# Output products by a seven-product scheme, with its sums on VectorE and a new order of the work

## The chip, the cores and the metric

The kernel runs on one core of one Trainium2 chip. The metric is the time of one execution in device microseconds. Engines are named as in the profile: PE (TensorE matmuls), PEld (its weight loads), DVE (VectorE), ACT (ScalarE), POOL (GpSimd), SP (SyncE, which here only issues DMAs).

## What is computed

Four items (batch entries), eight heads, 768 tokens of 64 values per head, eight blocks of 96 tokens. The reference, cut to what matters:

```python
P = sort_net                                   # 8x8 per head
for _ in range(5):                             # softmax over rows, then columns normalised
    P = exp(P - max(P)); P = P / sum(P, -1); P = P / sum(P, -2)
k_sorted, v_sorted = P @ blocks of k, P @ blocks of v
attn = softmax(q_block @ k_sorted_block.T / 8) # inside each block of 96
x    = attn @ v_sorted_block                   # 3072 tokens x 512
g    = maximum(x @ w1, x @ w2)                 # 3072 x 1024
out  = g @ w_out                               # 3072 x 512, float32
```

## The kernel before, in words

**The maxout is folded into the weights.** `w1_sb` is overwritten with w1 - w2, so that g = relu(x(w1 - w2)) + x w2, and out = relu(x(w1 - w2)) w_out + x (w2 w_out). `w_product` (L654) makes `wc` = w2 w_out once (512x512). Each 128 tokens of output are then twelve matmuls with 128 rows of contraction each: eight with `g` and `wo_sb`, four with `xT` and `wc`, all 512 columns wide (`out_products`, L700).

**Stages of an item b.** `load_k`, `load_q`, `load_v` (L132 to L172) are DMAs issued by POOL, in order, from float32 in memory to bf16 in SBUF. `sort_k` (L449, three calls) multiplies k by a block-diagonal matrix and evacuates to `kT`. `turn_v` (L242) copies v to another layout in `v_dc`, in four pieces of 24 columns. `sort_v_pair` (L516, eight calls, for items 1 and 2 together) and `sort_v_halved` (L493, four calls, for item 3) do for v what `sort_k` does for k. `pair_q` (L403, two DVE copies) and `q_transposes` (L413) make `qT`; for items 2 and 3 the transposes are DMAs on SP's queue. `scores` (L539, eight units u) does eight small matmuls and an exponential on ACT (L556). `values` (L567, eight units) does eight small matmuls and, on DVE, a reciprocal (L586) and a multiplication (L592). `x_transposes` (L600) makes `xT`; for items 1 to 3 these are DMAs on SP. `moe_h` (L685, two halves of 384 tokens, four pairs of 128 rows of g) does eight matmuls with 384 columns and a relu evacuation on ACT or DVE. `moe_out` (L714) does the twelve matmuls of a 128-token tile in two parts of six, evacuates two tiles together, and SP stores them (512 KB). `moe_out_last` (L729) does the last two tiles of the last item, the very last in pieces of 384 and 128 columns.

**PSUM.** One pool of four buffers (L62), each 128x1024 float32, that is two halves of 512 columns. Everything that PE writes takes one of the four, and gives it back when its evacuation has read it.

**The order of the work** is the order in which the program records instructions: each engine runs its own in that order and waits by semaphore. The front (L777 to L844), until item 0's g is there, is a list written out by hand. After it the loop at L915 runs, for each item, its eight `moe_h` units (item 0: none, but four `w_product`), then twelve half tiles of output, and after unit n the steps that `first_tail`, `second_tail`, `third_tail` (L859 to L914) give for n: the next item's attention. Which of ACT and DVE evacuates is chosen by `pick` (L96) from a running account of both, unless the step names one.

Of the kernel before, what the change touches and what calls it, by code (L numbers as in the profile page):

```python
# [10 lines left out]
FP32 = mybir.dt.float32  # L11
# [5 lines left out]
def kernel(  # L17
# [34 lines left out]
    NFB = DFF // 128  # L52
    NE = 8

# [77 lines left out]
    def load_q(b, by_pair=False):  # L132
        if b == 2:
            t = w2_sb.rearrange("p t f -> p (t f)")[:, 0 : H * R * D].rearrange(
                "p (h x) -> p h x", h=H
            )
        elif b == 3:
            t = v_raw[:, HB * D :].rearrange("p (h x) -> p h x", h=H)
        else:
            t = qpool.tile([128, H, R * D], BF16, tag="q_raw", name="q_raw", bufs=1)  # L140
        src = q[b].rearrange("h (p r) d -> p h (r d)", r=R)
        for hs in [slice(hp, H, HP) for hp in range(HP)] if by_pair else [slice(0, H)]:
            nc.gpsimd.dma_start(out=t[:, hs], in_=src[:, hs])
        q_raw[b] = t
# [7 lines left out]
    def load_k(b):  # L152
        k_raw[b] = (
            kpool.tile([128, HB * D], BF16, tag="k_raw", name="k_raw")
            if b < 3
            else v_raw[:, 0 : HB * D]
        )
        n = HB * D // NCH
        for ci in range(NCH):
            nc.gpsimd.dma_start(  # L160
                out=k_raw[b][:, ci * n : (ci + 1) * n],
                in_=k_src[b, :, ci * n : (ci + 1) * n],
            )
# [78 lines left out]
    def turn_v(rows, eng, c0, c1):  # L242
# [6 lines left out]
        else:  # L249
            nc.vector.tensor_copy(  # L250
                out=dst.bitcast(U32).rearrange("p (d c) -> p d c", c=BLK)[:, :, c0:c1],
# [150 lines left out]

    def pair_q(b, two):  # L403

        if two == 0:
            q_pair[b] = qpool.tile([128, HP, R, 2 * D], BF16, tag="q_pair", name="q_pair", bufs=1)
        nc.vector.tensor_copy(
            out=q_pair[b][:, :, :, two * D : (two + 1) * D],
            in_=q_raw[b][:, two * HP : (two + 1) * HP].rearrange("p h (r d) -> p h r d", r=R),
        )  # L410
        load["D"] += 900

# [123 lines left out]

    e_tiles, x_tiles = {}, {}

    def scores(b, u, n=0):  # L539
# [3 lines left out]
        for ii in range(4):  # L543
            i = ih * 4 + ii
            for h2 in range(2):
# [8 lines left out]
                )  # L554
        e = e_bufs[(b * 8 + u) % NE]
        nc.scalar.activation(  # L556
# [96 lines left out]

    def w_product(dmt):  # L654
        ps = ps_f32("wc_ps")
        for fb in range(NFB):
# [6 lines left out]
            )  # L663
        evac(wc[:, dmt, :], ps[:, 0:512], 512)

# [31 lines left out]

    out_ps = {}

    def out_products(dst, b, ti, n0=0, n1=512, part=None):  # L700
        ch, off = divmod(ti * 128, TCH)
        for m in range(NFB + HP) if part is None else range(part * 6, part * 6 + 6):
            hp = m - NFB
            nc.tensor.matmul(  # L704
                dst,
                g_tiles[b, ch, m // 2][:, m % 2, off : off + 128]
                if m < NFB
                else xT[:, b % 2, ch, hp % 2, hp // 2, off : off + 128],
                wo_sb[:, m, n0:n1] if m < NFB else wc[:, hp, n0:n1],
                start=(m == 0),  # L710
                stop=(m == NFB + HP - 1),
            )

    def moe_out(b, ti, part):  # L714
        slot = ti % 2
        if slot == 0 and part == 0:
            out_ps[0] = ps_f32("out_ps")
        ps = out_ps[0]
        out_products(ps[:, slot * 512 : (slot + 1) * 512], b, ti, part=part)
        if slot == 1 and part == 1:  # L720
            tok0 = b * S + ti * 128
            o = opool.tile([128, 2, 512], FP32, tag="o", name="o")
            evac(o.rearrange("p t n -> p (t n)"), ps, 1024)
            nc.sync.dma_start(
                out=out[tok0 - 128 : tok0 + 128, :].rearrange("(t p) n -> p t n", p=128),
                in_=o,
            )

    def moe_out_last(ti, pieces):  # L729

        tok0 = (B - 1) * S + ti * 128
        for n0, n1, eng in pieces:
            ps = ps_f32("out_ps")
            out_products(ps[:, 0 : n1 - n0], B - 1, ti, n0, n1)
            o = opool.tile([128, n1 - n0], FP32, tag=f"o{ti}{n0}", name="o", bufs=1)
            if eng == "A":
                nc.scalar.copy(out=o, in_=ps[:, 0 : n1 - n0])
            else:
                nc.vector.tensor_copy(out=o, in_=ps[:, 0 : n1 - n0])  # L739
            (nc.scalar if eng == "A" else nc.sync).dma_start(  # L740
                out=out[tok0 : tok0 + 128, n0:n1], in_=o
            )


    def att(b):

        SC = [lambda u=u: scores(b, u) for u in range(8)]
        VA = [lambda u=u: values(b, u) for u in range(8)]
        TR = [lambda t=t: x_transposes(b, t) for t in range(4)]
        return SC, VA, TR  # L750

# [94 lines left out]

    def turn(rows, c0):
        turn_v(rows, "D", c0, c0 + 24)
        load["D"] += 850

    def sorts_and_scores(b):
        SC, VA, TR = att(b)
        return SC, VA, TR, [lambda t=t: sort_k(b, t) for t in range(3)]

    SC, VA, TR, KS = sorts_and_scores(1)
    VS = [lambda t=t: sort_v_pair(2, t) for t in range(8)]
    TQ = [lambda half=half: q_transposes(1, half) for half in range(2)]
    TURN = [lambda c=c: turn(both, c) for c in (0, 24, 48, 72)]
    first_tail = {  # L859
        7: KS,  # L860
        9: [TQ[0], TURN[0]],
        10: [SC[0], TQ[1], TURN[1]],
        11: SC[1:4] + TURN[2:4] + [lambda half=half: load_v(3, half=half) for half in range(2)],
        12: VS[0:3],
        13: VS[3:6],
        14: VS[6:8] + [SC[4]],
        15: [VA[0], lambda: pair_q(2, 0)],
        16: [VA[1], lambda: pair_q(2, 1)],
        17: SC[5:8] + [TR[0]],
        18: [VA[2]],  # L870
        19: [VA[3], TR[1]],
        20: [VA[4]],
        21: [VA[5], TR[2]],
        22: [VA[6], VA[7], TR[3]],
    }
    SC, VA, TR, KS = sorts_and_scores(2)
    VS = [lambda t=t: sort_v_halved(3, t) for t in range(4)]
    TURN = [lambda c=c: turn(both, c) for c in (0, 24, 48, 72)]
    second_tail = {
        0: [lambda: q_transposes(2, 0), lambda: q_transposes(2, 1)],  # L880
        2: KS,
        4: SC[0:2],
        5: [VA[0]],
        6: SC[2:4] + [TURN[0]],
        7: [VA[1], TR[0]],
        8: [VA[2], TURN[1]],
        9: [VA[3], TR[1], TURN[2]],
        10: SC[4:7],
        11: [VA[4], TURN[3]],
        12: [VA[5], TR[2], lambda: load_k(3), lambda: load_q(3)],  # L890
        13: [VA[6]],
        14: SC[7:8] + VS[0:2],
        15: [VA[7], TR[3]],
        16: VS[2:4],
        17: [lambda: pair_q(3, 0)],
        18: [lambda: pair_q(3, 1)],
    }
    SC, VA, TR, KS = sorts_and_scores(3)
    third_tail = {
        0: [lambda: q_transposes(3, 0), lambda: q_transposes(3, 1)],  # L900
        2: KS,
        5: SC[0:2],
        6: [VA[0]],
        7: [VA[1], TR[0]],
        8: SC[2:5],
        9: [VA[2]],
        10: [VA[3], TR[1]],
        11: [VA[4]],
        12: SC[5:8],
        13: [VA[5], TR[2]],  # L910
        14: [VA[6]],
        16: [VA[7], TR[3]],
    }
    tails = [first_tail, second_tail, third_tail, {}]  # L914
    for b in range(B):  # L915
        units = [lambda ch=ch, t=t: moe_h(b, ch, t) for ch in range(2) for t in range(4)]
        cost = [13] * 8
        if b == 0:
            units, cost = [lambda: None] * 8, [0] * 8
        if b == 0:  # L920
            units += [lambda dmt=dmt: w_product(dmt) for dmt in range(4)]
            cost += [17] * 4
        units += [
            lambda ti=ti, part=part: moe_out(b, ti, part)
            for ti in range(6 if b < B - 1 else 4)
            for part in range(2)
        ]
        cost += [13] * 12
        if b == B - 1:
            units += [  # L930
                lambda: moe_out_last(4, [(0, 512, "D")]),
                lambda: moe_out_last(5, [(0, 384, "D"), (384, 512, "A")]),
            ]
        for n, unit in enumerate(units):
            elapse(100 * cost[n] if n < len(cost) else 0)
            unit()
            for step in tails[b].get(n, []):
                elapse(250)
                step()
# [28 lines left out]
```

## Time and profile before

| | |
|---|---|
| median of 3 runs | 166.83 us (166.24 to 167.07) |
| span of the profiled execution | 165.0 us |
| PE busy in it | 157.0 us (95%) |
| DVE, ACT, POOL busy | 77.5, 82.3, 33.9 us |
| mean granted TensorE clock | 0.999 |
| `out_ps` matmuls (L704) in the chain that ended last | 37% of the span |

The profiled execution's own time outside its span isn't recorded; the median of the runs is 1.83 us above the span. Busy times of PE are modelled and overlap, so the prediction goes by distances between starts. "a <-b" behind an idle time names what the engine waited for.

### The profile page before, as it was taken

What the parts mean: (1) busy time and instruction counts of PE and PEld (TensorE: products, weight loads), DVE (VectorE), ACT (ScalarE), POOL (GpSimd) and SP (SyncE); (2) the same over time, 40 slices, a digit from 0 to 9 for tenths busy, and PEclk for the clock granted to TensorE, in tenths of its full rate; (3) what the DMA queues carried; (4) which work ended last, traced back from release to release, by engine and by line L of the source; (5) the groups of instructions that cost most, each with busy time, mean ns of one, the idle gap of its engine ahead of it and who ended that gap; (6) DMA issues with size and microseconds to landing.
All of it is one profiled execution on the core that took longest, in us unless ns stands there. A gap on an engine that the chain in (4) does not pass through costs nothing.

```text
span 165.0 us, 4561 instructions
## 1 busy us (share of the span) xinstructions
PE 157.0 (95%) x2007; PEld 95.4 (58%) x2025; DVE 77.5 (47%) x170; ACT 82.3 (50%) x101; POOL 33.9 (21%) x61
## 2 busy tenths in 40 slices
PE   7889999999999999999999999999999999999992
PEld 7839776756554555557655554575655546654451
DVE  4878995684366564525277763250642420000011
ACT  3489776617239846055652353457447206642020
POOL 7949997131206000000014010000000000000000
PEclk9999999999999999999999999999999999999999
DMA  3999999999999999689515999995025294000333
GB/s 41 204 204 194 164 196 207 209 205 220 210 203 204 220 224 167 175 84 228 111 19 104 126 212 157 200 309 29 0 52 175 50 164 142 0 0 0 127 131 127
DMA packets 30404, 23.90 MB, mean 145 GB/s; under 512 B 16752, under 2 KB 25200, under 8 KB 30384
## 3 DMA queue, kind: packets, MB, share of 16 engines
q0 software_dynamic: 11040, 13.37, 50.0%
q1 hardware_dynamic: 19200, 10.17, 28.9%
q8 instruction: 16, 0.26, 0.7%
q10 hardware_dynamic: 144, 0.07, 0.1%
q14 instruction: 4, 0.03, 0.1%
HBM read 26.75 MB, written 6.29 MB: 200 GB/s over the span
## 4 chain that ended last, share of the span: by engine, by line
PE 81%; DMA 6%; DVE 5%; ACT 3%; POOL 2%; issue 2%
PE out_ps L704 37%; PE h_ps L677 25%; DMA w_sb<-in_moe_w_dram 5%; PE wc_ps L657 4%; PE o_ps L575 4%; PE k_ps L458 3%; PE s_ps L548 3%; ACT e L556 1%; POOL w_sb L189 1%; PE v_ps L523 1%; DMA p_sb<-in_sort_net_dram 1%; PE tq_ps L433 1%; DVE colsum L276 1%; DVE p_sb L273 1%; PE tw_ps L638 1%
## 5 line engine op out<-in xcount | busy, mean ns | idle before, releaser
L704 PE MATMUL out_ps<-wo_sb,g 128*128 128x512 bf16 (+2 forms) x187 | 46.0, 370 | 1.4 <-issue 1.0
L677 PE MATMUL h_ps<-xT,w_sb 128*128 128x384 bf16 x256 | 44.5, 326 | 0.0
L677 PEld LDWEIGHTS <-w_sb 128*128 128x128 bf16 x256 | 24.0, 98 | 15.5
L556 ACT ACTIVATE e<-s_ps 96x768 bf16<-96x768 f32 x32 | 24.0, 805 | 14.8 <-PE s_ps L548 14.8
L691 ACT ACTIVATE g<-h_ps 128x768 bf16<-128x768 f32 x27 | 21.7, 811 | 17.4 <-PE h_ps L677 17.3
L704 PEld LDWEIGHTS <-g 128*128 128x128 bf16 x200 | 17.1, 97 | 15.8
L704 PE MATMUL out_ps<-wc,xT 128*128 128x512 bf16 (+2 forms) x98 | 24.7, 370 | 0.1
L108 ACT COPY o<-out_ps 128x1024 f32<-128x1024 f32 x10 | 10.1, 1012 | 28.0 <-PE out_ps L704 25.2
L592 DVE TENSOR_TENSOR x<-o_ps,rs 96x512 bf16<-96x512 f32 x32 | 22.0, 687 | 1.1
L704 PEld LDWEIGHTS <-xT 128*128 128x128 bf16 x100 | 9.6, 97 | 11.2
L575 PEld LDWEIGHTS <-e 96*128 96x128 bf16 x256 | 11.7, 97 | 5.7 <-DVE v_sb L110 0.2
L586 DVE RECIPROCAL rs<-o_ps 96x8 f32<-96x8 f32 x32 | 6.4, 201 | 17.2 <-PE o_ps L575 17.1
L739 DVE COPY o<-out_ps 128x512 f32<-128x512 f32 (+1 forms) x2 | 1.2, 625 | 27.6 <-PE out_ps L704 27.6
L575 PE MATMUL o_ps<-v_sb,e 96*128 96x65 bf16 x256 | 12.7, 193 | 0.0
L110 DVE CAST kT<-k_ps 128x1024 bf16<-128x1024 f32 x6 | 7.2, 1222 | 8.4 <-PE k_ps L458 8.4
L110 DVE CAST v_sb<-v_ps 96x1024 bf16<-96x1024 f32 x7 | 8.5, 1219 | 4.9 <-PE v_ps L523 2.2
L160 POOL DMA_DIRECT2D v_raw<-in_k_dram x3 | 2.5, 838 | 35.1 <-DVE v_dc L250 31.4
L108 ACT CAST v_sb<-v_ps 96x1024 bf16<-96x1024 f32 x9 | 8.8, 1015 | 1.6 <-PE v_ps L500 0.8
L169 POOL DMA_DIRECT2D v_raw<-in_v_dram x11 | 6.5, 593 | 12.7 <-DVE v_dc L250 6.4
L693 DVE TENSOR_SCALAR g<-h_ps 128x768 bf16<-128x768 f32 x5 | 4.8, 957 | 8.9 <-PE h_ps L677 8.8
L548 PEld LDWEIGHTS <-kT 64*128 64x128 bf16 x256 | 6.1, 94 | 4.8 <-issue 2.6
L548 PE MATMUL s_ps<-qT,kT 64*128 64x96 bf16 x256 | 8.5, 204 | 0.3 <-DVE qT L110 0.2
(97 smaller groups left out, 144.4 us busy)
## 6 DMA issues: line engine op xcount, KB each, us to landing
out_dram<-o SPq DMA_DIRECT2D x11, 512.0 KB, 3.4
v_raw<-in_v_dram POOLq DMA_DIRECT2D x8, 384.0 KB, 13.5
k_raw<-in_k_dram POOLq DMA_DIRECT2D x9, 256.0 KB, 11.0
w_sb<-in_moe_w_dram POOLq DMA_DIRECT2D x4, 256.0 KB, 6.0
w_sb<-in_moe_w_dram POOLq DMA_DIRECT2D x2, 512.0 KB, 9.6
wo_sb<-in_moe_w_out_dram POOLq DMA_DIRECT2D x2, 512.0 KB, 13.7
v_raw<-in_v_dram POOLq DMA_DIRECT2D x3, 256.0 KB, 5.0
q_raw<-in_q_dram POOLq DMA_DIRECT2D x4, 192.0 KB, 9.1
```

Of the source, the lines that this page charges most:

```text
L108: nc.scalar.copy(out=out_ap, in_=in_ap)
L110: nc.vector.tensor_copy(out=out_ap, in_=in_ap)
L169: nc.gpsimd.dma_start(out=v_raw[r0 : r0 + 64, m * n : (m + 1) * n], in_=v_src[b, :, m * n : (m + 1) * n],)
L548: nc.tensor.matmul(ps[:, h2 * 512 + ii * 128 : h2 * 512 + ii * 128 + BLK], kT[b][rows, (hp * 8 + i) * BLK : (hp * 8 + i) * BLK + 128], rhs ...
L556: nc.scalar.activation(out=e[:, 0 : 8 * BLK].rearrange("p (t c r) -> p t c r", t=8, r=R), in_=ps[0:BLK] .rearrange("p (t f) -> p t f", t=8 ...
L575: nc.tensor.matmul(ps[:, h2 * 512 + ii * 65 : h2 * 512 + (ii + 1) * 65], e[:, (h2 * 4 + ii) * BLK : (h2 * 4 + ii) * BLK + 128], v_sb[:, m0 ...
L586: nc.vector.reciprocal(out=rs, in_=ov[:, :, :, 64])
L592: nc.vector.tensor_tensor(out=x, in0=ov[:, :, :, 0:D], in1=rs.to_broadcast([BLK, 2, 4, D]), op=ALU.mult,)
L657: nc.tensor.matmul(ps[:, 0:512], w2T[:, fb, dmt * 128 : (dmt + 1) * 128], wo_sb[:, fb, :], start=(fb == 0), stop=(fb == NFB - 1),)
L677: nc.tensor.matmul(h_ps[ch, t][:, m * 512 : m * 512 + TCH], w1_sb[:, hp, fb * 128 : (fb + 1) * 128], xT[:, b % 2, ch, hp % 2, hp // 2, :], ...
L691: nc.scalar.activation(out=g, in_=src, func=AF.Relu)
L704: nc.tensor.matmul(dst, g_tiles[b, ch, m // 2][:, m % 2, off : off + 128] if m < NFB else xT[:, b % 2, ch, hp % 2, hp // 2, off : off + 12 ...
```

## The change

The output rows of an item are split in halves `ch` (tokens 0 to 383, 384 to 767), the contraction of 1536 in halves (`g` pairs 0, 1 and half of `xT`; `g` pairs 2, 3 and the other half), and the 512 output columns in halves of 256 (`NW`). The four quarter products of each are replaced by seven products of sums (Strassen's algorithm, in Winograd's form). With A the left blocks, B the right ones, the sums are

S1 = A21 + A22, S2 = S1 - A11, S3 = A11 - A21, S4 = A12 - S2; T1 = B12 - B11, T2 = B22 - T1, T3 = B22 - B12, T4 = B21 - T2.

T is made once, from `wo_sb` (token `w0.n`, 128x1024 bf16) and `wc` (`w1.n`, 128x512); S for every item, from `xT` (`Xb.n`, 128x768) and from `g` (`Gb.t.n`, t = 0, 1, 128x768). All are tensor_tensor instructions on DVE. A group (class `Group`) has seven steps: `Pb.n` for tiles 0 and 1 of both halves, `Ub.n` for tile 2. It holds one PSUM buffer for all its steps and takes the two halves of it (`bank`) in turn; each step is six matmuls of 256 columns for each tile, and then a copy or an addition of PSUM and SBUF in float32. Stores of a group come after steps 5 and 6.

Other edits: `k_raw` of item 3 is now a buffer of the k pool, `q_raw` of item 3 lies in `v_dc`, and `q_pair` shares the storage of `q_raw`; so loads `lk3` and `lq3` are issued earlier and `lv0`, `lv1` (v of item 3) later, behind `y1`, a POOL copy of a few elements of item 1's `xT`, which waits for all four transposing DMAs of item 1. The exponentials rotate over six buffers and not eight. The order after the front is now one list of tokens: k, q, s, v, x, t, b, p, c, h are `sort_k`, `q_transposes`, `scores`, `values`, `x_transposes`, `turn_v`, sorts of v, `pair_q`, `w_product`, `moe_h` (numbers: item, then unit); a last letter A, D or P names ACT, DVE or POOL. The front is the same.

```diff
-    NE = 8
+    NE = 6
+    NW = DMODEL // 2
...
-            t = v_raw[:, HB * D :].rearrange("p (h x) -> p h x", h=H)
+            t = v_dc[:, 0 : H * R * D].rearrange("p (h x) -> p h x", h=H)
...
+        k_raw[b] = kpool.tile([128, HB * D], BF16, tag="k_raw", name="k_raw")
...
+            q_pair[b] = qpool.tile([128, HP, R, 2 * D], BF16, tag="q_raw", name="q_pair", bufs=1)
...
+    def product(self, bank, lw, rw, new):
+        n = 0
+        last = len(self.ks) * len(self.tiles) - 1
+        for k in self.ks:
+            for p, ti in enumerate(self.tiles):
+                ins = nc.tensor.matmul(
+                    self.ps[:, bank * 512 + p * NW : bank * 512 + (p + 1) * NW],
+                    left(self.b, lw, k, ti * 128), right(rw, k),
+                    start=new and n == 0, stop=n == last, ...)
+                self.apart(ins, bank)
+                n += 1
...
+    def step(self, at, eng):
+        if at == 0:
+            self.ps = ps_f32("out_ps")
...
+            self.product(0, "a11", "b11", True)
+            self.first = self.copy(self.by_tile(self.a), 0, eng)
+        elif at == 1:
+            self.product(1, 2, 2, True)
+            self.second = self.add(1, 0, 1, a, [self.first], eng)
+        elif at == 2:
+            self.product(0, "a12", "b21", False)
+            self.copy(self.part(0, 0), 0, eng)
+        elif at == 3:
+            self.product(1, 1, 1, False)
+            self.third = self.add(0, 1, 1, a, [self.first], eng)
+        elif at == 4:
+            self.product(0, 3, 3, True)
+            self.fourth = self.add(1, 1, 0, self.part(0, 1), [self.third], eng)
+        elif at == 5:
+            self.product(1, 4, "b22", False)
+            self.fifth = self.add(0, 1, 1, a, [self.first, self.fourth], eng)
+            self.store(0)
+        else:
+            self.product(0, "a22", 4, False)
+            self.add(1, 0, 0, self.part(1, 0), [self.first, self.second, self.fifth], eng, True)
+            self.store(1)
...
-    tails = [first_tail, second_tail, third_tail, {}]
-    for b in range(B):
...
+    plan = [
+        """
+        w0.1D k1.0A X0.1D G0.0.1D k1.1A X0.3D G0.1.1D c2D k1.2A lk3 X0.2D G0.0.2D w0.3D q1.0A
+        q1.1D c0D G0.1.3D G0.0.4D s1.0 s1.2 G0.1.2D G0.0.3D t1.0D t1.1D c3A t1.3D s1.4 s1.5
+        t1.2D c1A s1.6 s1.3 P0.0A b2.0A w0.2D w1.1D w1.2D b2.2A b2.7D P0.1D b2.4A b2.3A b2.1D
+        P0.2D b2.6A b2.5D k2.0A k2.1A k2.2A X0.4D w1.3D p2.0A G0.1.4D v1.0 p2.1D P0.3D v1.4 lq3
+        s1.7 q2.0 v1.2 P0.4D s1.1 U0.0A v1.7 U0.1D v1.5 U0.2A v1.6 U0.3D q2.1 v1.3 w0.4D x1.3
+        x1.2 w1.4D U0.4D v1.1 x1.0 x1.1 P0.5D k3.1A y1 P0.6D s2.5 s2.4 U0.5D U0.6D s2.6 s2.7
+        X1.1D lv1 k3.2A k3.0D lv0 h1.1.2D h1.1.1A X1.2D s2.2 s2.0 h1.1.3A p3.0D X1.3D h1.0.2A
+        v2.0 v2.4 h1.0.0A p3.1A G1.1.1D v2.5 h1.0.1A X1.4D x2.2 h1.1.0D G1.1.2D s2.1 s2.3
+        G1.0.1D h1.0.3A v2.1 G1.0.2D v2.7 P1.0A v2.6 U1.0D G1.1.3D G1.0.3D t3.1D P1.1D q3.0 v2.3
+        v2.2 x2.0 U1.1D t3.2D U1.2A q3.1 G1.1.4D P1.2A G1.0.4D P1.3D s3.4 s3.5 P1.4D x2.1 U1.3D
+        s3.7 t3.3D x2.3 s3.2 t3.0D P1.5D P1.6D U1.4D b3.3D s3.1 b3.1A U1.5D U1.6D b3.0D s3.6
+        b3.2D h2.0.2A h2.0.0A v3.5 v3.2 X2.1D h2.1.2A h2.1.3A X2.2D h2.1.0A v3.4 h2.0.1D G2.0.1D
+        h2.1.1A s3.0 G2.0.2D G2.0.4D G2.1.1D G2.1.2D s3.3 P2.0A U2.0A v3.6 v3.3 X2.4D P2.1D
+        h2.0.3A X2.3D U2.1D v3.7 x3.2 P2.2D U2.2A G2.1.3D G2.0.3D v3.1 v3.0 x3.1 x3.3 x3.0
+        G2.1.4D P2.3D P2.4D U2.3D U2.4D P2.5D U2.5D U2.6D P2.6D h3.1.0D h3.0.0A h3.1.2A G3.0.1D
+        h3.1.3A h3.0.1D G3.0.2D h3.1.1A X3.1D G3.0.3D G3.1.1D G3.1.2D h3.0.3A G3.1.3D U3.0D
+        h3.0.2A X3.2D P3.0A P3.1D G3.1.4D U3.1D U3.2D G3.0.4D P3.2A X3.4D X3.3D P3.3D P3.4D
+        U3.3D U3.4D P3.5D P3.6D U3.5D U3.6D
+        """,
+    ]
```

In `Group.add(ch, half, n, other, ...)` the output quarter (ch, half) is set to PSUM half n plus `other`; `apart` removes the ordering between PE's writes into one half of the buffer and reads of the other half.

## The prediction

> **What bounds the kernel now.** First the table by stage: the front ends at 38.4 us, and then come the tails of items 0, 1, 2 and 3 and the end. Columns: the stretch, its length, busy time and count of PE, PEld, DVE, ACT, POOL, then granted clock, DMA share and GB/s.
>
> ```profile
> 38.40:71.10 32.70, 31.88 (x498) 18.16 (x506) 18.34 (x29) 17.07 (x22) 3.55 (x5) 1.00 1.03 202
> 71.10:104.30 33.20, 32.58 (x422) 18.84 (x424) 17.74 (x28) 15.61 (x19) 3.40 (x4) 1.00 0.88 133
> 104.30:135.95 31.65, 31.43 (x359) 17.94 (x361) 11.30 (x21) 15.53 (x19) 0.00 (x0) 1.00 0.61 118
> 135.95:161.95 26.00, 25.86 (x146) 13.87 (x146) 1.25 (x2) 9.52 (x11) 0.00 (x0) 1.00 0.20 74
> 161.95:165.00 3.05, 0.00 (x0) 0.00 (x0) 0.00 (x0) 0.27 (x1) 0.00 (x0) 0.95 0.25 86
> ```
>
> PE is full in all four tails, at full clock; DVE and ACT are half idle. So PE work removed there is time, while DVE has 14 to 25 us per stage to give. Next, the chain of waits, in order of time:
>
> ```profile
> PE 81%; DMA 6%; DVE 5%; ACT 3%; POOL 2%; issue 2%
> ```
> ```profile
> 53.71 0.81 PE v_ps L523 x48
> 54.51 0.16 issue
> 54.67 1.24 PE out_ps L704 x5
> ```
>
> The chain lies on PE; its gaps are mostly such a 0.16 us step from matmuls on 64 rows (s, k, b) to full ones.
>
> **What PE saves.** The price of a matmul by its width is in the timeline of the last tiles (start, length, what); I read distances between starts:
>
> ```profile
> 158.27 1.03 PE L704 MATMUL out_ps<-wc,xT 128*128 128x512 bf16 x4
> ...
> 159.13 1.46 PE L704 MATMUL out_ps<-wo_sb,g 128*128 128x384 bf16 x8
> ...
> 160.43 0.81 PE L704 MATMUL out_ps<-wc,xT 128*128 128x384 bf16 x4
> ...
> 161.08 0.61 PE L704 MATMUL out_ps<-wo_sb,g 128*128 128x128 bf16 x8
> ...
> 161.53 0.39 PE L704 MATMUL out_ps<-wc,xT 128*128 128x128 bf16 x4
> 161.95 0.27 ACT L737 COPY o<-out_ps 128x128 f32<-128x128 f32 x1 [4.15 <-PE out_ps L704]
> 162.25 0.37 ACTq L740 DMA_DIRECT2D out_dram<-o  x1
> ```
>
> 0.86/4 = 215 ns at 512 columns, 1.30/8 = 162.5 at 384, 0.45/8 = 56 at 128, each with its own weight load: a line of 0.415 ns a column plus 3, even at 128. So 256 columns cost 109.4 ns. Before: 24 tiles x 12 x 216 = 62.2 us. After: 4 items x 7 products x 3 tiles x 6 = 504 x 109.4 = 55.1 us. **PE loses 7.1 us of work**; a P step is 1.31 us, a U step 0.66.
>
> [...]
>
> The rest of PE's list, by the chain's pieces: 9 k at 0.545, 4 c at 1.72, 2 q at 0.79, 24 s at 0.207, 12 b at 0.275, 24 v at 0.244, 24 h at 1.30: 58.7 us. Check on before: 58.7 + 62.2 = 120.9, and the last matmul ended at 161.93, 123.5 after 38.4; 2.6 us are gaps, at 17 such steps 0.15 each. The new list has 20 steps: 3.1. So with nothing else late PE ends at 38.4 + 58.7 + 55.1 + 3.1 = 155.3.
>
> **What DVE gains.** Its prices, from the groups (busy, mean ns | idle) and DVE's timeline:
>
> ```profile
> L231 DVE TENSOR_TENSOR w_sb<-w_sb 128x1024 bf16<-128x1024 bf16 x2 | 1.3, 688 | 0.3 <-DMA w_sb<-in_moe_w_dram 0.3
> ...
> L739 DVE COPY o<-out_ps 128x512 f32<-128x512 f32 x1 | 0.7, 692 | 26.3 <-PE out_ps L704 26.3
> ```
> ```profile
> 59.88 0.20 DVE L586 RECIPROCAL rs<-o_ps 96x8 f32<-96x8 f32 x1
> 60.12 0.69 DVE L592 TENSOR_TENSOR x<-o_ps,rs 96x512 bf16<-96x512 f32 x1
> 60.73 0.55 DVE L407 COPY q_pair<-w_sb 128x1536 bf16<-128x1536 bf16 x1
> ```
>
> A bf16 sum of 1024 takes 688 ns; copies from PSUM of 512 and 1024 (692 and 1224) give a start of about 155 ns, so 768 take 155 + 533 x 3/4 = 555 and 512 take 422. An addition from PSUM to float32 isn't in the trace: 690 for 512 columns, as the copy and as L592 (687, also two operands); 425 for 256. That makes 48 S sums 26.6 us, 8 T sums 4.4, P and U steps on DVE 25.0; PE's work hides them as long as DVE keeps pace, and rival 2 has the price if it doesn't. With all the rest the list puts 100.7 us on DVE beside 113.8 on PE, 62.3 beside 62.3 up to U1.6 (about 101 us), hardly less than PE there. But a length isn't what the next instruction waits: 60.12 to 60.73 is 0.61 for a length of 0.69, so 0.08 less, and a reciprocal with its product 0.845, not 0.888. Of 105 instructions in that stretch 73 save 0.08 and 16 pairs 0.043: **55.8 us of DVE beside 65.5 of PE** (62.3, 18 steps of 0.15, and 0.5 of the waits below). DVE's largest lead over PE, 4.7 us of lengths (at v1.1), falls to 1.3. ACT has 60 us in all; at 20.7 against 19.1 (k2.2, p2.0) it is the fuller one for a moment.
>
> **New waits of PE.** I walked the list with these prices, each engine in its own order. While P and U of an item are open, two of four PSUM buffers are left. k2.1 and k2.2 wait for buffers that ACT empties (0.2 each), U0.0 waits 0.25 for s1.7's, which stands on ACT behind p2.0. Elsewhere there is cover: P0.1's sums 0.1 us, t1.2 before b2.0 almost none, P1.3 after P1.1's addition 3.3. That is 0.7 us. Bounds: nothing (the gaps above may already hold it) to 4.7 (DVE's lead, unshortened). I take 1.5, nearest the walk. PE ends at **156.8**.
>
> SP: each item's stores stand behind the transposes of the next, and x2.2 and q3.0 behind stores; scores s3.4 need q3.0 about 93, which I place at 91. POOL: lk3 waits for k1's sort, lq3 for b2's, with only loads behind them. Gate y1 opens when x1's transposes have landed, about 75.5; behind it stand the four 384 KB pieces of v, for t3.1 at about 88.8. Such pieces took 9.9 us after 49.3 (median): 78.5 (last issue) + 9.9 = 88.4. Just in time; so nothing (rival 3 has the price). The shared storage costs nothing either: p2.0 comes 15 us after q1's transposes have read `q_raw`; lq3's load into `v_dc`, issued about 57.5, has 18 us until p3.0 against 10.5 for the same load before (the row `v_raw<-in_q_dram`); of the six exponential buffers each has been read by its `values` before its next `scores` in the list.
>
> **The end.** Before, the last 64 KB went out at 162.25, landed in 1.7, and the span closed 3.05 after PE's end E. After, P3.5, P3.6, U3.5, U3.6 store 512, 512, 256, 256 KB, the first from E - 1.85. Rates by fortieths of 100 to 165 us:
>
> ```profile
> GB/s 107 193 302 182 178 327 294 57 12 0 0 0 131 0 0 129 315 0 112 14 319 95 40 247 76 0 0 0 0 0 0 0 19 304 0 10 321 163 136 25
> ```
>
> No slice passes 327. At 320, first bytes 0.75 after the issue (157.83, the 321 slice begins 158.5), the bytes run from E - 1.1 for 4.9 us to E + 3.8; landing 0.5 later and the old 1.05 to close make E + 5.3: **2.3 us lost**. Were they not queued: the last addition ends at E + 0.5, 256 KB land in 2.0: E + 3.55. I take 5.3; the rate row is the nearer.
>
> **Sum.** Span 156.8 + 5.3 = 162.1, against 165.0; with the 1.83 us by which the median stands above the span, **163.9 us**, 2.9 less.
>
> **Rivals.**
> 1. Gaps only, stores not queued: 155.3 + 3.55 + 1.83 = 160.7. For: each cover holds on paper. Against: the 320 GB/s.
> 2. The other side: DVE becomes the bound up to U1.6. If instructions cost their lengths and the 24 S and 4 small T sums there run at L592's rate (1.04 ns an element, +0.40 and +0.27 each, 10.7 us), DVE needs 73.0, 7.5 more than PE's 65.5: 171.4. It decides from 68.4 us, when the 2.9 are gone: 0.12 more on each of 105 instructions than my 55.8. Against: L231 shows 1024 in 688. Half of it, an unshortened lead of 4.7: 167.1.
> 3. Late v. Behind t3.1 on DVE stands P1.1's addition; PE notices 3.3 us later. If pieces land by the trace's slowest, 17.0: 95.5, 3.4 past 92.1: 167.3.
> 4. The products don't get cheaper (weight loads paced at 128 columns or more): the 56 ns row excludes it; no chance of its own.
>
> **Chances.** Forecast (162 to 165.5) 0.55; rival 1 0.15; DVE half 0.10; DVE whole 0.12; late v 0.08. The range 160.6 to 167.6 holds all but the whole DVE case. A measurement tells about 0.5% (166.0, 167.7) from no change: faster 0.72 (forecast, rival 1 and a little of the others), same 0.15, slower 0.13.
>
> **What would show it.** Right: L804 matmuls 109 ns apart, PE's stages shorter by some 1.8 us an item, DVE's busiest stretch below nine tenths of PE's, PE's end near 157 and 5 us from there to the span's end. Wrong: PE waiting for DVE's additions (L830) or sums (L734, L750); 768-element sums near 955 ns; t3 (L247) waiting for v_raw's DMA; pairs of weight load and matmul further apart than 109 ns.

## The result, and the profile after

| | before | after |
|---|---|---|
| median on the same chip | 166.76 us | 165.12 us |
| ratio after/before (95%) | | 0.9885 (0.9843 to 0.9927) |
| profiled execution: time, span | not recorded, 165.0 us | 165.25, 163.1 us |
| last matmul ends | 161.93 us | 158.28 us |
| from there to the span's end | 3.05 us | 4.8 us |
| time outside the span | 1.83 us (median against span) | 2.15 us |

Four runs each; one of the four of after, 166.96 us, counts as slow, and the ratio leaves it out while the median doesn't. The forecast was 163.9 us in a range of 160.6 to 167.6: the direction and the range hold, and 1.2 us of the forecast gain are missing. PE's front still ends at 38.35 us. The sum by stage goes wrong in the first tail. The same columns as before (stretch, length, busy time and count of PE, PEld, DVE, ACT, POOL, clock, DMA share, GB/s), of after:

```profile
38.40:71.00 32.60, 29.83 (x624) 22.32 (x623) 26.32 (x49) 22.09 (x28) 3.38 (x5) 1.00 1.07 177
71.00:101.00 30.00, 30.00 (x437) 22.66 (x436) 24.36 (x51) 16.90 (x23) 2.27 (x5) 1.00 0.98 184
...
105.00:128.00 23.00, 23.00 (x282) 17.34 (x273) 18.50 (x36) 10.71 (x15) 0.00 (x0) 1.00 0.26 81
128.00:158.00 30.00, 30.00 (x246) 23.81 (x244) 18.38 (x35) 6.04 (x8) 0.00 (x0) 1.00 0.19 69
158.00:163.10 5.10, 0.27 (x3) 0.00 (x0) 0.50 (x2) 0.00 (x0) 0.00 (x0) 0.86 0.66 256
```

From 71 us on PE is never idle for long. Up to 71 us it lacks 2.8 us, with DVE at 26.3 of 32.6: not DVE's pace. PE's own waits name no engine (line, what was waited for, total, times, longest):

```profile
PE out_ps L804 <- issue: 2.0, 1, 2.0
...
PE k_ps L456 <- issue: 0.6, 1, 0.6
```

"Issue" is time in which PE waited for nothing that the profile shows. The two places in PE's timeline (start, length, what, idle before):

```profile
56.98 0.38 PE L456 MATMUL k_ps<-bd,k_raw 64*64 64x64 bf16 x12
57.97 1.51 PE L456 MATMUL k_ps<-bd,k_raw 64*64 64x64 bf16 x84 [0.62 <-issue]
...
61.80 0.42 PE L574 MATMUL o_ps<-v_sb,e 96*128 96x65 bf16 x8
64.17 1.03 PE L804 MATMUL out_ps<-wt_early,g 128*128 128x256 bf16 x8 [1.95 <-issue]
65.04 0.60 PE L804 MATMUL out_ps<-w2T,sums_x 128*128 128x256 bf16 x4
```

The first stop lies in the middle of `k2.0`, between two matmuls of one step with equal operands; the k that they read had landed at 52.56, so no data is late there. The second lies ahead of the products of `P0.4`, after their first weight load (62.02). PE runs 113.8 us of work from 38.35 to 158.28, so 6.1 us are gaps: 2.57 in these two stops, and 3.6 that are nearly all steps between row counts (the forecast had 3.1 for those). No wait for a PSUM buffer is among PE's waits: the 84 matmuls behind the first stop start 16 ns apart, to 59.30.

**A clue in the counts.** Listed in PE's own order, weight loads and matmuls together, the rows at which PE stops are 1979 and 2235: 256 apart. The profile has a queue that it calls "instruction" (queue, packets, MB, share of 16 engines). After, then before:

```profile
q8 instruction: 17, 0.28, 0.7%
```
```profile
q8 instruction: 16, 0.26, 0.7%
```

16 KB a packet. After has 2229 weight loads and as many matmuls, 17.4 times 256 rows, for 17 packets; before has 2025 weight loads, so about 4050 rows, 15.8 times 256, for 16. So a packet fits a block of 256 rows of PE. Products now come in matmuls of 256 columns and not 512, 109 ns apart and not 215, so while it runs products PE uses up a block (128 pairs of weight load and matmul) in 14.0 us and not 27.5.

### The profile page after: what moved, and what is told of

Read it like the earlier page. It is cut to its first block, busy times and chain, and to the rows that moved or that the text cites. A ratio compares the mean times of both kernels' runs of the same rounds, so it can differ in the third digit from the quotient of the medians.

```text
span 163.1 us, 5109 instructions
## 1 busy us (share of the span) xinstructions
PE 152.8 (94%) x2229; PEld 116.4 (71%) x2229; DVE 120.7 (74%) x263; ACT 81.5 (50%) x104; POOL 32.6 (20%) x62
## 4 chain that ended last, share of the span: by engine, by line
PE 80%; DMA 6%; DVE 5%; issue 2%; POOL 2%; ACT 2%; ACTq 0%
PE out_ps L804 35%; PE h_ps L676 25%; DMA w_sb<-in_moe_w_dram 6%; PE wc_ps L656 4%; PE o_ps L574 4%; PE s_ps L546 3%; PE k_ps L456 3%; PE v_ps L521 1%; POOL w_sb L186 1%; ACT kT L109 1%; PE tq_ps L431 1%; DMA p_sb<-in_sort_net_dram 1%; DVE colsum L273 1%; PE v_ps L498 1%; DVE p_sb L270 1%
## 5 line engine op out<-in xcount | busy, mean ns | idle before, releaser
L830 DVE TENSOR_TENSOR o<-out_ps,a 128x512 f32<-128x512 f32 (+1 forms) x24 | 13.2, 552 | 5.5 <-PE out_ps L804 2.6
L804 PEld LDWEIGHTS <-sums_g 128*128 128x128 bf16 x144 | 13.6, 98 | 1.7
L830 DVE TENSOR_TENSOR o<-out_ps,o 128x512 f32<-128x512 f32 (+1 forms) x16 | 8.9, 558 | 6.4 <-PE out_ps L804 6.1
L804 PE MATMUL out_ps<-wo_sb,g 128*128 128x256 bf16 x96 | 13.1, 273 | 0.0
L109 ACT CAST kT<-k_ps 128x1024 bf16<-128x1024 f32 x10 | 9.8, 1018 | 5.6 <-PE k_ps L456 5.6
L804 PE MATMUL out_ps<-w2T,sums_x 128*128 128x256 bf16 x72 | 11.8, 273 | 0.0
L804 PEld LDWEIGHTS <-sums_x 128*128 128x128 bf16 x96 | 8.9, 98 | 1.3
L692 DVE TENSOR_SCALAR g<-h_ps 128x768 bf16<-128x768 f32 x7 | 6.7, 956 | 3.3 <-PE h_ps L676 3.2
L804 PE MATMUL out_ps<-wt_early,g 128*128 128x256 bf16 x48 | 6.5, 272 | 2.0 <-issue 2.0
L456 PEld LDWEIGHTS <-k_raw 64*64 64x64 bf16 x384 | 6.6, 110 | 2.0 <-issue 1.9
```

The source lines that it names most:

```text
L109: nc.scalar.copy(out=out_ap, in_=in_ap)
L456: nc.tensor.matmul(ps[r0 : r0 + 64, m * 64 : (m + 1) * 64], kv[r0 : r0 + 64, t * 16 + m, :], bd_k[b][r0 : r0 + 64, :], start=True, stop=True,)
L692: nc.vector.tensor_scalar(out=g, in0=src, scalar1=0.0, scalar2=None, op0=ALU.max)
L804: ins = nc.tensor.matmul(self.ps[:, bank * 512 + p * NW : bank * 512 + (p + 1) * NW], left(self.b, lw, k, ti * 128), right(rw, k), start=n ...
L830: ins = nc.vector.tensor_tensor(out=self.part(ch, half), in0=self.by_tile(self.bank(n)), in1=other, op=ALU.add)
```

## Experiments

**Theory A:** PE's instructions arrive in blocks of 256, by the queue above, whose packets the profile counts on the same 16 DMA engines as the loads (0.7% of their time). While item 3's loads of k and q fill these (1.07 DMA share above), a block takes longer to come than PE takes to run one, and PE stops. **Rivals (B):** a hidden wait for data or buffers at those places; DVE's new work; the order of the list itself. What the chain loses at the end is a matter by itself. Ratios are to the kernel before on the same chip, whose medians there were 166.2 to 166.5 us; kernels that ran on different chips are compared by them. That of after is 0.9885.

### q's load behind the stop

```diff
+elif kind == "z":
+    nc.gpsimd.tensor_copy(out=held, in_=x_tiles[1, 1, 0][:, 0, 0, 0, 0:2])
-P0.3D v1.4 lq3
+P0.3D v1.4 z1 lq3
```

> The changed kernel, and the load of item 3's q (768 KB) held back by a POOL copy that waits for item 1's v1.4, so that it is issued at about 63 and not at 55.4 us. Theory A: PE's two stops without a semaphore (0.62 us in k2.0, 1.95 us before P0.4, exactly 256 instructions apart) are its own instructions arriving late, in blocks of 256, behind the packets of that load. Then both go or shrink to under 0.5 us together, PE ends near 156.3 and the time is 1.5 to 2.2 us under the changed kernel's, about 163.2. Theory B: the stops are waits for DVE or a PSUM buffer that the profile doesn't name. Then they stay, and the time is the changed kernel's, 165.1, or more if p3.0 now waits for q.

Measured: 166.41 us, ratio 0.9943 (0.9904 to 0.9982). The profiled execution took 167.07 us, more than the median; its places are used, not its length. The stop ahead of P0.4 is gone, that in `k2.0` stays (0.60 us, up to 57.42; the load's new place is at 62.91), and a new wait is there:

```profile
61.24 0.42 PE L574 MATMUL o_ps<-v_sb,e 96*128 96x65 bf16 x8
61.50 1.04 PE L804 MATMUL out_ps<-wt_early,g 128*128 128x256 bf16 x8
...
75.83 0.52 PE L546 MATMUL s_ps<-qT,kT 64*128 64x96 bf16 x16 [2.70 <-DMA qT<-q_pair]
```

The load moved on top of the DMAs that transpose q of item 2. The chain of waits has them at 11.85 us:

```profile
63.94 11.85 DMA qT<-q_pair
```

So A holds for the second stop alone. Its time of 163.2 doesn't hold: what the stop gave was lost, with more, to the collision. The stop in `k2.0` isn't that load's doing.

### The same products, other block borders

```diff
-keep_streaming(ps_f32("fill_ps"), 92 * 118, most=118)
+keep_streaming(ps_f32("fill_ps"), 92 * 118, most=512)
```

This filler of the front, which only keeps PE running, is 22 pieces in place of 92: 140 PE instructions fewer, all ahead of 38 us, and not one edit near the stops.

> The changed kernel with the filler matmuls at the very start cut into 22 pieces of up to 512 columns and not 92 of 118 (the same columns in all), so that every later PE instruction stands 140 places earlier and the blocks of 256 end at other instructions. Theory A (late instruction blocks): no stop before P0.4; the stops, if any, are 140 instructions later in the list: within k2.2 and within the U0 steps about v1.6, of 0 to 2 us. Theory B (a wait for another engine): the 1.9 us before P0.4 stay where they are. The time: A 163.5 to 165.1, B 165.1.

Measured: 164.19 us, 0.9871 (0.9841 to 0.9902); span 161.8, PE's end 157.08.

```profile
62.70 0.42 PE L574 MATMUL o_ps<-v_sb,e 96*128 96x65 bf16 x8
62.96 1.04 PE L804 MATMUL out_ps<-wt_early,g 128*128 128x256 bf16 x8
```
```profile
PE v_ps L477 <- issue: 1.2, 1, 1.2
PE o_ps L574 <- issue: 1.0, 1, 1.0
```

Both old stops are gone. The two new ones aren't where the expectation had them (`k2.2`, U0) but in the front, at 17.85 and 24.87 us, beside the front's loads (with the front of after, the DMA share is 1.35 from 14 to 18 us and 1.24 from 22 to 25). By PE's rows they stand at 446 and 702, again 256 apart, and within three rows of where steps of 256 back from 1979 lead (443, 699). A wait for data or DVE at `k2.0` or `P0.4` would have stayed. That excludes the first rival.

### Long stores first at the end

```diff
-U3.3D U3.4D P3.5D P3.6D U3.5D U3.6D
+P3.5D P3.6D U3.3D U3.4D U3.5D U3.6D
```

> The changed kernel with the last steps in the order P3.3 to P3.6, then U3.3 to U3.6, so that the two 512 KB stores are issued 1.3 us earlier. Theory A: the end is bound by the bytes of the last four stores (1.57 MB at the 403 GB/s of the profile, 3.9 us from 0.8 after the first issue): from PE's end to the span's end 3.8 to 4.1 us and not 4.8, the time 0.7 to 1.0 us less, 164.2. Theory B: the end is bound by the last addition and a fixed latency of the last store: 4.8 stays, and U3.5 and U3.6 wait for additions of U3.3 and U3.4 (their cover is 0.66 us for 0.42 plus the semaphore): 0 to 0.3 us more.

Measured: 164.64 us, 0.9882 (0.9835 to 0.9928); span 161.1. PE's end to the span's end is 3.84 us, 1 us shorter. The last addition stands right behind PE's end in both, so the end isn't its doing. After, then this kernel, from the chains of waits:

```profile
158.31 0.42 DVE o L830
```
```profile
157.26 0.42 DVE o L830
```

Both old stops are there (0.60 and 1.68 us). The profiles gain 2.0 us of span, 1.0 of it at the end. Against before on its chip no gain in time is shown: 0.9882 beside after's 0.9885, with runs from 162.78 to 165.31.

### Without most of the sums

```diff
+elif kind in "XG" and n[0] > 0:
+    pass
```

> The changed kernel without the S sums of items 1 to 3 (36 of 48 DVE sums left out, so the output of these items isn't the reference's). Theory A: DVE's sums are hidden behind PE. The time is the changed kernel's within 0.5 us. Theory B: DVE's load (88% of PE's up to U1.6) is what costs the rest of the gain: 1.5 us or more less, 163.5 or under.

Measured: 165.52 us, 0.9937 (0.9907 to 0.9967); span 164.2. Not faster, and the stops are the same:

```profile
PE out_ps L804 <- issue: 2.0, 1, 2.0
```

36 sums (about 20 us of DVE) cost nothing, so DVE isn't the bound there. They all come behind 76 us in after; the 12 sums of item 0, beside the stops, are still made. That the stops aren't DVE's follows from the runs that move or remove them with DVE's work as it was: the moved borders above, and the loads left out below. Together these take the second rival away.

### Other borders again, with the new end

```diff
-keep_streaming(ps_f32("fill_ps"), 92 * 118, most=118)
+keep_streaming(ps_f32("fill_ps"), 92 * 118, most=236)
```

and the edit of the end, as above.

> The changed kernel with the two edits of the first four runs that shortened it or may: the last steps in the order P3.3 to P3.6, U3.3 to U3.6, and the filler at the start in 46 pieces and not 92, which puts every later PE instruction 92 places earlier and so the ends of PE's blocks of 256 instructions at other places than with 92 or 22 pieces. Theory A (end bound by bytes, stops from late instruction blocks): 3.8 us from PE's end to the span's end, no stop before P0.4, stops of 0 to 2 us together elsewhere; time 162.5 to 164.5. Theory B (the 1 us of the other order was a chance of the run): 4.8 us at the end.

Measured: 164.18 us, 0.9878 (0.9847 to 0.9909); span 162.0, PE's end 158.22. No stop at k2.0 or P0.4; one of 1.97 us in the front and one of 0.37 at `o_ps`:

```profile
17.66 0.63 PE L431 MATMUL tq_ps<-ident,q_raw 128*64 128x128 bf16 x15 [1.97 <-issue]
```
```profile
PEclk9999879999999999999999999999999999999999
```

The stop in the front, up to 17.66 us, lies beside the front's loads, as that up to 17.85 with 22 pieces does; that these loads cause it, no run shows. Behind the stop the granted clock of two slices falls to 0.8 and 0.7. A border moved is luck, not a cure.

### The list, the gate and the loads alone

`Group.step` issues a seventh of the plain products (twelve matmuls of 512 columns a tile, 288 in all), each tile is copied by DVE, and no sums are made. List, gate, storage and loads stay.

> The list, the gate and the loads of the changed kernel, but plain products: the seven steps of a group are sevenths of its twelve matmuls of 512 columns per tile (the half of the later tokens first), each tile evacuated by one DVE copy, no sums at all. Theory A: the seven products are worth the 7.1 us of PE work less what they bring; with 2 x 256 columns for 512 the blocks of 256 instructions last twice as long in the products, so that the two stops go too, and the end stores less at once. So PE's end 155.7 + 7.1 = 162.8, the end 3 to 4 us, the time 167.5 to 169. Theory B: the gain over the kernel before comes from the list and the loads: 165 or less.

Measured: 168.84 us (168.75 to 168.86), 1.0151 (1.0123 to 1.0180); span 166.8, PE's end 162.71. No stop of that kind is longer than 0.22 us, and the clock is full throughout. That is 2.7 us more than before on its chip (166.18), and after is 1.6 less than before on its own. The seven products therefore gain about 4.3 us of the 7.1 that PE's work shrinks, and list and loads alone cost 2.7. The third rival has that share, but not the stops: with half the rate of instructions, the same list and loads give none.

### Without the gate

```diff
-P0.3D v1.4 lq3
+P0.3D v1.4 lq3 lv1 lv0
-P0.5D k3.1A y1 P0.6D
+P0.5D k3.1A P0.6D
```

and `lv1`, `lv0` taken out farther on.

> The changed kernel without the gate: the four loads of item 3's v are issued right behind that of its q, at about 57 us and not at 78. Theory A: 1.6 MB more keep the DMA engines full until about 72, and what is small and urgent comes late: instruction blocks (another stop of 1 to 2 us about 74), q2's transposes (2 to 4 us before s2.5) and x1's (before h1.1.2). Time 167 to 170. Theory B: none of it is late, since v is needed only at 100 and transposes have slack: 165.1, or less, as the transposes of items 2 and 3 then meet no loads.

Measured: 166.49 us, 0.9984 (0.9956 to 1.0013): beside after's 0.9885 the gate is worth about 1.0%, 1.6 us. How long SP's queue was on the transposes of item 2's q, in after and in this kernel:

```profile
62.80 4.12 SPq L417 DMA_TRANSPOSE qT<-q_pair  x2
```
```profile
62.43 10.19 SPq L417 DMA_TRANSPOSE qT<-q_pair  x2
```

PE then waits 0.80 us in the scores of item 2, and both stops remain (0.50 and 1.95). The profiled span is 0.6 us longer (163.7 for 163.1); where the rest of the 1.6 lies isn't shown.

### Without item 3's loads of k and q

```diff
-load_k(3)
+k_raw[3] = k_raw[2]
-load_q(3)
+q_raw[3] = q_raw[2]
```

> The changed kernel with the loads of item 3's k and q left out (k and q of item 2 are used in their place, so item 3's output isn't the reference's). Theory A: without the 1.6 MB in the DMA queues from 44 to 65 us both stops, in k2.0 and before P0.4, shrink under 0.3 us together, q2's transposes aren't late, and PE ends near 155.7: time 162.3 to 163. Theory B: the stops are not the loads': 165.

Measured: 162.88 us (162.34 to 163.18), 0.9791 (0.9763 to 0.9820); span 160.2, PE's end 155.44. PE's instructions and the borders of their blocks are those of after. PE's longer waits:

```profile
PE fill_ps L83 <- DVE fill L74: 1.2, 1, 1.2
PE tw_ps L637 <- DMA w_sb<-in_moe_w_dram: 0.3, 1, 0.3
PE k_ps L456 <- ACT v_sb L109: 0.2, 1, 0.2
PE pe L353 <- DVE p_bf L275: 0.2, 1, 0.2
PE s_ps L546 <- DVE qT L111: 0.2, 1, 0.2
```

No stop is left, and PE ends 2.84 us earlier: the 2.57 of the stops, and 0.3 that the front's wait for `w_sb` can explain (0.3 us here, 0.7 in after). The ratios differ by 0.9%, 1.6 us; the two profiled spans by 2.9. With the moved borders and the plain products this settles the cause: these stops need both a block's end at that place and the loads beside it.

### k's load behind the gate

`lk3` moves from behind `k1.2A` to behind `y1`, `lv0` to beside `lv1`, the three sorts of k behind `v2.7`; with the new end.

> The changed kernel with its last steps in the order P3, then U3 (worth 1 us at the end by the run that did it alone), and the load of item 3's k (three pieces, 0.8 MB) moved from 44 us to behind the gate at 77.5, ahead of v's pieces; its three sorts move behind v2.7. Theory A: the DMA engines then run dry about 53 and q's load is done by about 61, so that the blocks of 256 instructions come in time: no stop in k2.0, under 0.5 us before P0.4; v lands about 92, in time for t3.1 at 92. PE ends near 155.7, the time is 161.5 to 162.5. Theory B (a load moved means another collision, as with q's load behind v1.4): q3's transposes meet the loads of k and v and s3.4 or k3 waits 1 to 3 us; 163 to 165.

Measured: 166.03 us, 0.9965 (0.9934 to 0.9997); a miss. The stop in k2.0 is gone, that of P0.4 stays (1.69 us), and k now lies on the loads of v and the transposes of q of item 3:

```profile
86.40 9.90 SPq L417 DMA_TRANSPOSE qT<-q_pair  x1
```

The scores of item 3 wait 0.48 and 1.33 us for them.

### q's load behind the gate

```diff
-P0.3D v1.4 lq3
+P0.3D v1.4
-P0.5D k3.1A y1 P0.6D
+P0.5D k3.1A y1 lq3 P0.6D
```

with `p3.0D` behind `G1.1.2D`, `p3.1A` behind `h1.0.3A`, and the new end.

> The same order at the end, and the load of item 3's q moved behind the gate in place of k's (p3.0 and p3.1 come 8 us later in the list). Theory A: the stop before P0.4 goes (its block is fetched from 57.5, when no load is left), the 0.6 in k2.0 stays, q2's and x1's transposes meet no load: PE's end 156.3. But q lands about 86, its transposes meet v's loads and s3.4 at 97 has none of the cover that k has: 0 to 2 us. Time 162 to 164.5. Theory B: stops stay at 2.6 us: 164.2.

Measured: 163.52 us, 0.9833 (0.9810 to 0.9856), the fastest of those that do the whole work; four runs between 163.47 and 163.65, the fifth 166.03. PE's end is 157.62, 3.8 us from there to the span's end.

```profile
57.71 1.51 PE L456 MATMUL k_ps<-bd,k_raw 64*64 64x64 bf16 x84 [0.58 <-issue]
...
96.13 0.52 PE L546 MATMUL s_ps<-qT,kT 64*128 64x96 bf16 x16 [0.35 <-DMA qT<-q_pair]
...
99.87 0.51 PE L546 MATMUL s_ps<-qT,kT 64*128 64x96 bf16 x16 [1.15 <-DMA qT<-q_pair]
```

The two single moves, and the first experiment, show which load belongs to which stop: k's to k2.0, q's to P0.4. Each move pays a part back to the transposes.

## Why the prediction was right or wrong

- **Width of the products: right.** 64.17 to 65.04 is 0.87 for eight matmuls, 109 ns as predicted. The plain kernel prices the lot: PE's end 162.71 there, 155.44 without stops here, 7.27 apart, against 7.1 predicted (the two differ in item 3's loads as well).
- **DVE: right.** The sums took 543 to 559 ns (555 predicted), and the additions what the copies did (690 and 425 predicted):

```profile
L830 DVE TENSOR_TENSOR o<-out_ps,a 128x512 f32<-128x512 f32 x12 | 8.2, 687 | 4.7 <-ACT a L839 2.5 <-PE out_ps L804 2.1
L830 DVE TENSOR_TENSOR o<-out_ps,a 128x256 f32<-128x256 f32 x12 | 5.0, 418 | 0.8 <-PE out_ps L804 0.5 <-issue 0.3
...
L750 DVE TENSOR_TENSOR sums_g<-g,sums_g 128x768 bf16<-128x768 bf16 x8 | 4.3, 550 | 0.0
```

- PE waits for no sum and no addition, and without the later sums nothing is faster. In the first tail DVE has 26.3 us beside 29.8 of PE, 88%. Rival 2 is out.
- **Gate and v: right, by more than "just in time".** The gate opened at 77.48 (75.5 predicted), the last load of v was issued at 79.5 and landed at 91.74, and t3.1 started at 94.19, where 88.8 was placed, without waiting. Rival 3 is out in this kernel.
- **New waits: the step that failed.** "I take 1.5" summed waits for buffers only. Of those at most 0.4 showed: without the stops PE's end would be 155.7, and gaps alone make 155.3. The 2.57 us of late instructions weren't in any term: I counted what PE's instructions cost to run, never how fast they come. PE's end is 158.28 and not 156.8. Without the loads that fill the DMA engines it is 155.44, just where rival 1's "gaps only" has it (155.3). That the total still came so near is partly luck: some 1.1 us taken for buffers that nobody waited for paid for nearly half of the stops.
- **The end: queueing right, rate misread.** Stores do queue behind each other, but at about 405 GB/s and not 320. The rates of 150 to 163 us of after, in fortieths:

```profile
GB/s 0 0 0 0 0 0 0 0 0 0 0 0 0 0 0 0 0 0 0 0 0 0 139 410 403 410 397 410 416 403 403 410 403 410 227 0 0 0 0 0
```

- The bytes went out from 157.35 to 161.36, 0.9 us before PE's end to 3.1 behind it, where 3.8 was forecast; the closing took 1.7 and not 1.55. That makes 4.8 us and not 5.3. The 320 came from reading a mean as a ceiling: a slice of the forecast's row is 1.6 us wide, and 321 GB/s over it is 0.52 MB, one whole store of 512 KB, which is out in less than a slice. In slices of 0.15 us (157 to 163 us of before) the same lone store runs at 355 to 410 GB/s, no slower than four in a queue:

```profile
GB/s 109 0 0 0 0 0 0 0 0 0 0 164 396 396 410 396 355 382 410 396 191 0 0 0 0 0 328 396 410 341 273 0 0 0 0 0 0 0 276 379
```

- **The sum.** PE's end +1.5, the tail -0.5: the span is 163.1, not 162.1. The time outside the span is 2.15 in the profiled run, about 2.0 in the others, 0.1 to 0.3 over the 1.83 taken. All three make 165.25; the median is 0.13 lower.

**The price of a block.** Counted back 256 rows from the first stop, PE entered the block ahead of it at 52.34 and ran it in 5.0 us, to 57.36; it could go on at 57.97, 5.6 us after 52.34. The block ahead of the second stop it ran from 57.97 to 62.02, 4.1 us, and went on at 64.17, 6.2 us after 57.97. The trace of after also has a 16 KB packet of the instruction queue ahead of the end of each stop. They began at 55.70 and 61.86, 3.4 and 3.9 us after PE had entered the block before, and took 0.9 and 1.1 us; PE went on 1.3 us after the end of each. The DMA share up to these starts was 1.27 (52.34 to 55.70) and 1.23 (57.97 to 61.86), with 0.70 and 0.72 MB of loads. With no load in the queues (72.17 to 73.07, share 0.86, transposes) a packet began 0.9 us after PE had entered the block before. So beside those loads the packet starts late; its own transfer takes 0.9 to 1.3 us anywhere in after.

The two stops are 2.57 us together. Nor is that a fixed price of two blocks: with 22 filler pieces PE ran a block in 3.8 us (56.58 to 60.40) beside the same loads, and PE didn't stop.

**Open.** What holds the start of a packet back, by 0.9 to 4.4 us in the first twelve of after: the loads have a part, but the exception above shows that they aren't all of it. How far ahead a block is asked for: each of those twelve packets starts after PE has entered the block before, which fits one block ahead, but no run changes it. The clock's dips (0.60 to 0.84 in slices of 4 us) stand next to stops in three of the traces; that the stops cause them is not shown. Of the 2.7 us that list and loads cost with plain products, the profiles place 0.8 in PE's end (162.71 for 161.93) and 1.0 behind it (4.1 for 3.05); why wasn't tried.

## What to carry to other kernels

A change that halves the work of each instruction nearly doubles the rate at which an engine uses up its program (here a product's weight load and matmul every 109 ns and not 215): count instructions per microsecond, and set 256 of them (weight loads count too) against the time in which a block comes while loads run, here 5.6 and 6.2 us at the two stops. A stop marked "issue" in the middle of one step, at rows 256 apart, is likely that; moving the loads or the borders tells it from a data wait, and the packets of the instruction queue show when the block came. Before a load is moved out of one engine's way, look for the transposing DMAs that it will land on.

## What the runs showed of the hardware that was not expected

- Blocks of 256 instructions come late beside loads: stops of 0.4 to 2.0 us, at other places after 140 instructions fewer, none in the run without item 3's loads of k and q. At both stops of after PE went on 1.3 us after the end of the packet.
- After some stops PE's granted clock sank for a while, after others of the same length it didn't: 0.84 and 0.74 in the two slices of 4 us behind the 1.97 us stop of the kernel with 46 filler pieces, 0.60 at 64 to 68 us behind the 1.96 us stop of that without most of the sums, 0.65 there behind 1.69 us with k's load moved; but 1.00 there behind 1.95 us in after. With plain products and no such stop the clock was 1.000 and four runs agreed within 0.11 us.
- The transposing DMAs of q landed 4.9 to 7.5 us after their issue in after; where a load was put beside them, the chain of waits had 11.85 us of them (q's load behind the stop), and SP's queue was on them for 10.19 us (no gate; 4.12 in after) and, on one alone, 9.90 (k's load behind the gate; 3.88 in after).
- Stores of 256 and 512 KB go out at 397 to 416 GB/s with four queued, and a lone one of 512 KB at 355 to 410; a slice wider than the store hides this.
